# A retention block and a bilinear FFN in one kernel: the first regular group's queries and keys transposed by DMA instead of on TensorE, with the loads around it reordered

## The chip, the cores and the metric

The kernel runs on one core of a Trainium2 chip. The metric is the device time of one execution in microseconds (us). Before the change it is 326.99 us, the median of three runs (326.97 to 328.62).

## The reference

Inputs are q, k and v of shape [8, 8, 576, 64] (batch, heads, sequence, head dimension) and three FFN weights. The retention part computes scores, multiplies them with a causal decay, and applies them to v; there is no softmax. Its output, 4608 tokens of 512 channels, goes through a bilinear FFN.

```python
scores = scale * np.matmul(q, k.transpose(0, 1, 3, 2))
gamma = 1.0 - 2.0 ** (-5.0 - np.arange(H, dtype=np.float32))
Dmat = np.where(rel >= 0, gamma[:, None, None] ** rel[None, :, :], 0.0)
attn = np.matmul(scores * Dmat[None], v)          # [B, H, S, D]
x = attn.transpose(0, 2, 1, 3).reshape(B * S, H * D)
out = ((x @ w_a) * (x @ w_b)) @ w_out             # 512 -> 1536 -> 512
```

## The kernel before

**The FFN is the stream that everything else is woven into.** The 4608 tokens are worked off in blocks of 512, 256, 256 and then 512 tokens (line 111). For one block `ffn_block` runs, for each of 12 slices F of the hidden dimension, four matmuls into `pa` (L748) and four into `pb` (L763). ACT copies pa out of PSUM as `ha` (L756), and DVE multiplies ha with pb into `hT` (L768). Then, for each 128 tokens of the block (u = 0, 1, ...), twelve matmuls with `wo_sb` make `po` (L782), which ACT (L791) or DVE (L793) copies into an output buffer `osb`. There are four osb buffers. SP, the DMA queue of SyncE, stores them (L704, L706).

**Retention.** Tokens come in 18 groups of 256. Groups 0 to 2 are done in half-size steps at the start (STEPS, `transpose_step`, `score_step`, `output_step`); from group 3, the first regular one (FIRST = 3), each group passes these stages:

- `load_pair(n, which)` (L148): for q, k and v two DMAs of 256 KB each on SP's queue, into float32 stage tiles qf, kf, vf.
- `ahead(n)`: POOL casts q and k to bf16 `qkb` (L469, L473) and scales v into `vb` (L474).
- the transposition of qkb into `qkT`: by `turn(n)`, two transposing DMAs on SP's queue, one for q and one for k (L501); or, for group 3 alone, by `turned(3, part)`, four steps of four transposing matmuls on PE each (L492) into a PSUM tile of the FFN's own pool, and a copy to SBUF on ACT or DVE (L494).
- `stretch(into, outof)`: on PE, the states' part of the output of group `outof` (L627), the key-value sums of group `into` (`keyed`, L537, needs qkb and vb), its scores (`matched`, L599, needs qkT), and the keys' part of the output of `outof` (L640). DVE adds the sums (L562), masks the scores (L608) and scales the output into `xT` (L650), the FFN's input; ACT converts the states (L566, L569, L573). These are queued in `later` and emitted by `pop()` between FFN steps. `open_alone` and `close_outputs` do the two output parts without a new group.

**What sets the order.** The order is written by hand. `todo` is a list of (place, function, arguments); the place is counted in units of a 512-column matmul chain of PE from the FFN's start, so the first block takes 0 to 144, the second 144 to 216, the third 216 to 288, the fourth 288 to 432. At each edge of `ffn_block` all entries whose place has come are emitted, in the order of their places. Every engine, and SP's queue, works its instructions strictly in that order. So an entry that waits on SP also holds the loads and stores that stand behind it.

Two buffers matter for the change. The first block's four osb tiles are stored partly late: those of u = 0, 2 and 3 are put into `held` and stored by `store_held` entries, that of u = 1 is stored at once. The next block's osb tiles take the buffers that these stores free. And qkT has three buffers, as have qkb and vb.

Of the kernel before, what the change touches and what calls it, by code (L numbers as in the profile page):

```python
# [11 lines left out]
BF16 = mybir.dt.bfloat16  # L12
# [6 lines left out]
def kernel(  # L19
# [10 lines left out]
    nc = tc.nc  # L30

    B, H, S, D = q.shape
    DM = H * D
# [4 lines left out]
    HP = H // 2  # L38
# [8 lines left out]
    FIRST = 3  # L47
# [16 lines left out]
    def rows_of(n):  # L64

        if n not in LEFT:
            b, m = PAIRS[n]
            return [(kp, 0, 128, b, 256 * m + 128 * kp) for kp in (0, 1)]
        return [(i // 2, 64 * (i % 2), 64, 4 * LEFT[n] + i, S - 64)
                for i in range(4)]  # L70

    def pool(name, bufs, space=None):
        kw = {} if space is None else {"space": space}
        return ctx.enter_context(tc.tile_pool(name=name, bufs=bufs, **kw))
# [6 lines left out]
    qkt_pool = pool("qkt", 3)  # L81
# [7 lines left out]
    ps_ffn = pool("ps_ffn", 4, PS)  # L89
# [50 lines left out]
    def load_pair(n, which=(0, 1, 2)):  # L140
        if n >= NP:
            return
        paired.setdefault(n, {})
        for i in which:
            name, src = (("qf", q), ("kf", k), ("vf", v))[i]
            t = stage.tile([128, 2 * DM], FP32, tag=name, name=name + "2")
            for kp, r0, m, b, s0 in rows_of(n):
                nc.sync.dma_start(  # L148
                    t[r0:r0 + m, kp * DM:(kp + 1) * DM]
                    .rearrange("p (h d) -> p h d", h=H),  # L150
                    src[b, :, s0:s0 + m, :].rearrange("h s d -> s h d"))
            paired[n][i] = t

    def load_step(n, hh, which, on=nc.sync):

        if n not in paired:
            paired[n] = [stage.tile([128, 2 * DM], FP32, tag=name, name=name)
                         for name in ("qf", "kf", "vf")]
        on.dma_start(  # L159
            paired[n][which][:, hh * DM:(hh + 1) * DM]  # L160
            .rearrange("p (h e) -> p h e", h=4),
            (q, k, v)[which][n, 4 * hh:4 * hh + 4, 0:256, :]
            .rearrange("h (p two) d -> p h (two d)", two=2))

    STEPS = [(0, 0), (1, 0), (0, 1), (1, 1), (2, 0), (2, 1)]
    Q, K, V = 0, 1, 2
# [12 lines left out]
    identity = const.tile([128, 128], BF16)  # L179
# [49 lines left out]
    def pair_tables(step):  # L229
# [17 lines left out]
        else:  # L247
# [6 lines left out]
                for n in range(FIRST)]  # L254
    second = sum_pool.tile([128, FIRST, HP, 64], FP32, tag="sums",
                           name="second")
# [16 lines left out]
    natural, transposed, scored = {}, {}, {}  # L273
# [205 lines left out]
            op=ALU.mult)  # L479
        natural[FIRST + n, "pair"] = (qkb, vb)  # L480

    def turned(n, part):

        qkb = of(natural, n)[0]
        if part == 0:
            transposed[FIRST + n, "pair"] = qkt_pool.tile(
                [128, 2, 2, HP, 128], BF16, tag="qkT", name="qkT2")
        w, kp = part // 2, part % 2
        tp = ps_ffn.tile([128, HP, 128], BF16, tag="ab", name="tp2")
        for c in range(HP):  # L490
            e0 = kp * DM + c * 128
            nc.tensor.transpose(tp[:, c, :], qkb[:, w, e0:e0 + 128], identity)  # L492
        copy = (nc.scalar.copy, nc.vector.tensor_copy)[kp]
        copy(of(transposed, n)[:, w, kp], tp)  # L494

    def turn(n):
        qkb = of(natural, n)[0]
        qkT = qkt_pool.tile([128, 2, 2, HP, 128], BF16, tag="qkT",
                            name="qkT2")
        for w in (0, 1):  # L500
            nc.sync.dma_start_transpose(  # L501
                qkT[:, w].rearrange("p k c s -> p (k c) s"), qkb[:, w])
        transposed[FIRST + n, "pair"] = qkT
        if n == 9:
            load_pair(n + 1, (K, V))
        if n >= 9:
            load_pair(n + 2)

    def of(store, n):
        return store[FIRST + n, "pair"]  # L510
# [373 lines left out]
    nc.sync.dma_start(gate, wo_sb[0:1, 3, 0:64])  # L884
    for i, which in ((4, Q), (4, K), (4, V), (5, Q), (5, K), (5, V)):
        load_step(*STEPS[i], which)
    for n in (FIRST, FIRST + 1):
        load_pair(n)
    load_pair(FIRST + 2, (Q,))

# [20 lines left out]
    def turn_step(i):  # L913
# [3 lines left out]
    todo = [(100, early_casts, ()), (112, turn_step, (4,)),  # L917
            (112.1, cast_step, (5, Q, "act")), (116, score_step, (4,)), (116, state_step, (4,)),
            (124, turn_step, (5,)), (128, output_step, (4,)),
            (128, score_step, (5,)), (128, state_step, (5,)),  # L920
            (140, output_step, (5,))]
# [1 line left out]
    todo += [(136, total_of, (2,))]  # L923
    todo += [(28 + 6 * step, pair_tables, (step,)) for step in range(13)]
    todo += [(170, stretch, (3, None)), (197, stretch, (4, 3)),
             (240, stretch, (5, 4)), (272, open_alone, (5,)),
             (276, close_outputs, (5,)), (336, stretch, (6, None)),
             (372, stretch, (7, 6)), (408, stretch, (8, 7))]
    for n in range(8, NP, 2):
        todo += [(starts[n] - 116, stretch, (n + 1, n)),  # L930
# [2 lines left out]
                 (starts[n] - 44, open_alone, (n + 1,))]  # L933
    todo += [(starts[NP - 2] - 40, close_outputs, (NP - 1,))]
    placed = {args[0]: at for at, fn, args in todo if fn is stretch}
    casts = {3: 116, 4: 116, 5: 141, 6: 200, 7: 250, 8: 330}
    turns = {4: 116, 5: 145, 6: 240, 7: 338, 8: 345}
    loads = {7: 212, 8: 271, 9: 345.1}
    todo += [(345.2, load_pair, (10, (Q,))),
             (145.1, load_pair, (6, (K,))),  # L940
             (145.2, load_pair, (6, (Q,))), (145.3, load_pair, (6, (V,)))]
    for n in range(9, NP):
        casts[n], turns[n] = placed[n] - 70, placed[n] - 38
    todo += [(156 + 3 * part, turned, (3, part)) for part in range(4)]
    for fn, places in ((ahead, casts), (turn, turns), (load_pair, loads)):
        todo += [(at, fn, (n,)) for n, at in places.items()]
    todo += [(116, load_pair, (5, (K,))), (116, store_held, ()),
             (116, load_pair, (5, (V,))), (145, store_held, ())]
    todo.sort(key=lambda e: e[0])

    at = 0.0
# [40 lines left out]
```

## Time and profile before

| What | Value |
|---|---|
| Median of three runs | 326.99 us (326.97 to 328.62) |
| The profiled execution's own time | 327.43 us |
| Span of its instructions | 325.7 us |
| PE busy (matmul) | 319.4 us, 98% |
| DVE / ACT / POOL busy | 161.8 / 129.4 / 116.8 us |
| Granted TensorE clock | 1.0 in every stage |
| DMA, mean over the span | 155 GB/s; 66.7% of 16 engines in the main queue |
| SP's waits for stores of osb (L706 on ACT's copies) | 91.5 us in 13 waits |

All durations below are of the profiled execution. Times on the axis are counted from the start of its span. A matmul's busy time overlaps that of the next, so PE's timeline shows a group of four 256-column matmuls as 0.60 us although the next group starts 0.44 us later; the chain of waits shows the 0.44. A releaser (what an instruction waited for) is inferred from the last semaphore event; where the named one had long been done, it was another, often a DMA. For a DMA the profile tells when SP issued it, how long the issue held SP, and how long after the issue's start it landed.

### The profile page before, as it was taken

What the parts mean: (1) busy time and instruction counts of PE and PEld (TensorE: products, weight loads), DVE (VectorE), ACT (ScalarE), POOL (GpSimd) and SP (SyncE); (2) the same over time, 40 slices, a digit from 0 to 9 for tenths busy, and PEclk for the clock granted to TensorE, in tenths of its full rate; (3) what the DMA queues carried; (4) which work ended last, traced back from release to release, by engine and by line L of the source; (5) the groups of instructions that cost most, each with busy time, mean ns of one, the idle gap of its engine ahead of it and who ended that gap; (6) DMA issues with size and microseconds to landing.
All of it is one profiled execution on the core that took longest, in us unless ns stands there. A gap on an engine that the chain in (4) does not pass through costs nothing.

```text
span 325.7 us, 8666 instructions
## 1 busy us (share of the span) xinstructions
PE 319.4 (98%) x3615; PEld 165.1 (51%) x3615; DVE 161.8 (50%) x289; ACT 129.4 (40%) x286; POOL 116.8 (36%) x150
## 2 busy tenths in 40 slices
PE   7899999999999999999999999999999999999996
PEld 3564458768544554544454545454445444444443
DVE  5734455666446663845374626561556245314421
ACT  6845753563435523533253324442333233213321
POOL 4990078550876182757075205440520000000000
PEclk9999999999999999999999999999999999999999
DMA  8999999999999999996999169926840500031013
GB/s 216 254 197 207 262 225 223 191 176 202 221 220 221 215 231 198 209 210 152 194 199 189 51 159 200 217 62 149 206 67 31 140 28 0 2 97 32 3 29 100
DMA packets 143175, 50.37 MB, mean 155 GB/s; under 512 B 124576, under 2 KB 138656, under 8 KB 143136
## 3 DMA queue, kind: packets, MB, share of 16 engines
q1 hardware_dynamic: 137856, 44.84, 66.7%
q0 software_dynamic: 4752, 4.72, 8.8%
q8 instruction: 28, 0.46, 0.6%
q10 hardware_dynamic: 528, 0.26, 0.3%
q14 instruction: 11, 0.09, 0.1%
HBM read 37.75 MB, written 9.44 MB: 145 GB/s over the span
## 4 chain that ended last, share of the span: by engine, by line
PE 94%; DMA 2%; SPq 2%; ACT 1%; DVE 0%; issue 0%; DVEq 0%; ACTq 0%
PE po L782 29%; PE pb L763 29%; PE pa L748 28%; DMA qf<-in_q_dram 2%; SPq L159 2%; PE o L627 2%; PE o L640 2%; PE sc L599 1%; PE kv L537 1%; PE pa L725 1%; PE o L427 0%; PE kv L368 0%; PE sc L343 0%; PE tp L492 0%; PE tp L328 0%
## 5 line engine op out<-in xcount | busy, mean ns | idle before, releaser
L768 DVE TENSOR_TENSOR hT<-ha,pb 128x512 bf16<-128x512 bf16 (+1 forms) x120 | 75.9, 634 | 98.1 <-PE pb L763 90.9
L756 ACT CAST ha<-pa 128x512 bf16<-128x512 f32 (+1 forms) x120 | 64.8, 543 | 119.6 <-PE pa L748 116.4
L763 PE MATMUL pb<-xT,wb_sb 128*128 128x512 bf16 (+1 forms) x480 | 111.5, 358 | 0.3 <-ACT osb L791 0.3
L748 PE MATMUL pa<-xT,wa_sb 128*128 128x512 bf16 (+1 forms) x468 | 108.8, 357 | 0.0
L782 PE MATMUL po<-wo_sb,hT 128*128 128x512 bf16 (+2 forms) x444 | 97.5, 374 | 0.0
L763 PEld LDWEIGHTS <-wb_sb 128*128 128x128 bf16 x480 | 46.9, 98 | 47.0 <-issue 0.7
L748 PEld LDWEIGHTS <-wa_sb 128*128 128x128 bf16 x468 | 44.9, 98 | 44.3 <-issue 0.2
L782 PEld LDWEIGHTS <-hT 128*128 128x128 bf16 x444 | 41.9, 98 | 47.2
L469 POOL CAST qkb<-qf 64x1024 bf16<-64x1024 f32 x15 | 15.5, 1031 | 75.3 <-DMA qf<-in_q_dram 74.3
L474 POOL TENSOR_TENSOR vb<-vf,vs 128x1024 bf16<-128x1024 f32 x15 | 28.5, 1902 | 11.5 <-DMA vf<-in_v_dram 5.2
L793 DVE COPY osb<-po 128x512 f32<-128x512 f32 (+1 forms) x16 | 10.9, 683 | 39.7 <-PE po L782 39.7
L791 ACT COPY osb<-po 128x512 f32<-128x512 f32 (+1 forms) x21 | 12.0, 571 | 45.2 <-PE po L782 44.7
L650 DVE TENSOR_TENSOR xT<-o,qs 128x512 bf16<-128x512 f32 x30 | 19.5, 683 | 5.2 <-PE o L640 5.2
L562 DVE TENSOR_TENSOR sums<-kv,sums 128x256 f32<-128x256 f32 x44 | 18.6, 424 | 2.8 <-PE kv L537 0.8
L469 POOL CAST qkb<-kf 64x1024 bf16<-64x1024 f32 x15 | 15.8, 1052 | 11.4 <-DMA kf<-in_k_dram 10.8
L608 DVE TENSOR_TENSOR sT<-sc,mask 128x512 bf16<-128x512 f32 x30 | 19.5, 682 | 0.0
L473 POOL CAST qkb<-kf 64x512 bf16<-64x512 f32 x30 | 17.7, 616 | 0.8
L473 POOL CAST qkb<-qf 64x512 bf16<-64x512 f32 x30 | 17.6, 616 | 0.6
L566 ACT CAST states<-sums 64x512 bf16<-64x512 f32 x26 | 16.0, 617 | 0.3
L311 POOL CAST qkb<-kf 128x512 bf16<-128x512 f32 x5 | 3.1, 617 | 16.6 <-DMA kf<-in_k_dram 16.6
L667 ACT COPY fence<-o 128x2 f32<-128x2 f32 x15 | 2.4, 160 | 16.4 <-PE o L627 16.4
L809 PE MATMUL w<-ones 128*128 128x512 bf16 x19 | 7.0, 486 | 1.5 <-DVE idxp_f L204 1.5
(87 smaller groups left out, 163.1 us busy)
## 6 DMA issues: line engine op xcount, KB each, us to landing
qf<-in_q_dram SPq DMA_DIRECT2D x32, 256.0 KB, 5.2
vf<-in_v_dram SPq DMA_DIRECT2D x32, 256.0 KB, 5.1
kf<-in_k_dram SPq DMA_DIRECT2D x31, 256.0 KB, 4.9
out_dram<-osb SPq DMA_DIRECT2D x25, 256.0 KB, 2.9
out_dram<-osb SPq DMA_DIRECT2D x20, 128.0 KB, 2.4
wo_sb<-in_moe_w_out_dram POOLq DMA_DIRECT2D x3, 512.0 KB, 16.3
qf<-in_q_dram SPq DMA_DIRECT2D x8, 128.0 KB, 3.2
kf<-in_k_dram SPq DMA_DIRECT2D x8, 128.0 KB, 3.6
```

The source lines that it names most:

```text
L469: nc.gpsimd.tensor_copy(qkb[0:64, w], t[0:64])
L473: nc.gpsimd.tensor_copy(to[:, :, 1 - r], fro[:, :, r])
L474: nc.gpsimd.tensor_tensor(vb.rearrange("p (k h d) -> p k h d", k=2, h=H), vf.rearrange("p (k h d) -> p k h d", k=2, h=H), vs2[:, 2 if n in ...
L562: nc.vector.tensor_tensor(sums[:, i], own, prev, op=ALU.add)
L566: nc.scalar.copy(to(half(1 - r)), fro(half(r)))
L608: nc.vector.tensor_tensor(sT[:, on].rearrange("p c k s -> p (c k) s"), sc[:, on].rearrange("p c k s -> p (c k) s"), mask3.unsqueeze(1).to_ ...
L650: nc.vector.tensor_tensor(x_of(t0, 128).rearrange("p c (a s) -> p c a s", a=2), o[:, :, :, kp].rearrange("p a c s -> p c a s"), qs[:, :, s ...
L748: nc.tensor.matmul(pa[:, 0:n], wa_sb[:, c, fs], xT[:, c], start=(c == 0), stop=(c == NC - 1))
L756: nc.scalar.copy(ha[:, 0:n], pa[:, 0:n])
L763: nc.tensor.matmul(pb[:, 0:n], wb_sb[:, c, fs], xT[:, c], start=(c == 0), stop=(c == NC - 1))
L768: nc.vector.tensor_tensor(hT[:, F, 0:n], has[F][:, 0:n], pb[:, 0:n], op=ALU.mult)
L782: nc.tensor.matmul(po[:, 0:width], hT[:, F, u * 128:(u + 1) * 128], wo_sb[:, F, cols], start=(F == 0), stop=(F == NF - 1))
```

## The change

Group 3 is no longer transposed on PE: `turned` is deleted, and `turn(3)` puts two transposing DMAs on SP's queue at place 116. Because SP works in order, the loads around it are placed anew:

- Before the FFN's first block only group 3 and group 4's q are loaded ahead. Group 4's k and v come after `turn(3)`, then `turn(4)`, then group 5's q and k, the first `store_held`, and group 5's v.
- SP's order from group 3's loads on was: q3 k3 v3, q4 k4 v4, q5, turn 4, k5, store of u = 0, v5, store of u = 1, turn 5. It becomes: q3 k3 v3, q4, turn 3, store of u = 1, k4 v4, turn 4, q5 k5, store of u = 0, v5, turn 5.
- The stretch of groups 5 and 4 moves from place 240 to 248, two FFN slices later. `open_alone(5)` and `close_outputs(5)` move from 272 and 276 to 274 and 278; since the next edges are 276 and 280, each comes four po matmuls later.
- `turn(7)` moves from 338 to 272. On SP it then stands right after group 8's q, and group 8's k and v come after it, with one output store between.

```diff
-    def turned(n, part):
...
-        tp = ps_ffn.tile([128, HP, 128], BF16, tag="ab", name="tp2")
-        for c in range(HP):
-            e0 = kp * DM + c * 128
-            nc.tensor.transpose(tp[:, c, :], qkb[:, w, e0:e0 + 128], identity)
-        copy = (nc.scalar.copy, nc.vector.tensor_copy)[kp]
-        copy(of(transposed, n)[:, w, kp], tp)
...
-    for n in (FIRST, FIRST + 1):
-        load_pair(n)
-    load_pair(FIRST + 2, (Q,))
+    load_pair(FIRST)
+    load_pair(FIRST + 1, (Q,))
...
-             (240, stretch, (5, 4)), (272, open_alone, (5,)),
-             (276, close_outputs, (5,)), (336, stretch, (6, None)),
+             (248, stretch, (5, 4)), (274, open_alone, (5,)),
+             (278, close_outputs, (5,)), (336, stretch, (6, None)),
...
-    casts = {3: 116, 4: 116, 5: 141, 6: 200, 7: 250, 8: 330}
-    turns = {4: 116, 5: 145, 6: 240, 7: 338, 8: 345}
-    loads = {7: 212, 8: 271, 9: 345.1}
-    todo += [(345.2, load_pair, (10, (Q,))),
+    casts = {3: 116, 4: 116.15, 5: 141, 6: 200, 7: 250, 8: 330}
+    turns = {3: 116, 4: 116.2, 5: 145, 6: 240, 7: 272, 8: 345}
+    loads = {7: 212, 9: 345.1}
+    todo += [(345.2, load_pair, (10, (Q,))), (271, load_pair, (8, (Q,))),
+             (272.1, load_pair, (8, (K, V))),
...
-    todo += [(156 + 3 * part, turned, (3, part)) for part in range(4)]
...
-    todo += [(116, load_pair, (5, (K,))), (116, store_held, ()),
-             (116, load_pair, (5, (V,))), (145, store_held, ())]
+    todo += [(116.1, load_pair, (4, (K, V))), (116.3, load_pair, (5, (Q, K))),
+             (116.4, store_held, ()), (116.5, load_pair, (5, (V,))),
+             (145, store_held, ())]
```

More of the change, by code (lines that the diff above doesn't have):

```diff
@@ L480, in ahead @@
         natural[FIRST + n, "pair"] = (qkb, vb)
-    def turned(n, part):
[L484 to L488, printed above, removed]
-        tp = ps_ffn.tile([128, HP, 128], BF16, tag="ab", name="tp2")
-        for c in range(HP):
-            e0 = kp * DM + c * 128
-            nc.tensor.transpose(tp[:, c, :], qkb[:, w, e0:e0 + 128], identity)
-        copy = (nc.scalar.copy, nc.vector.tensor_copy)[kp]
-        copy(of(transposed, n)[:, w, kp], tp)
     def turn(n):
```

## The prediction

> **What bounds the kernel now.** I read part 1 of the page first: PE is busy almost all the span.
>
> ```profile
> PE 319.4 (98%) x3615; PEld 165.1 (51%) x3615; DVE 161.8 (50%) x289; ACT 129.4 (40%) x286; POOL 116.8 (36%) x150
> PE 94%; DMA 2%; SPq 2%; ACT 1%; DVE 0%; issue 0%; DVEq 0%; ACTq 0%
> ```
>
> The second line, the chain that ended last, says the same: 94% of it is matmuls. So an edit is worth what it takes from, or puts into, PE's stream. I then asked for the chain between 50 and 80 us, where the diff acts (start, duration, what):
>
> ```profile
> 53.31 0.22 PE tp L492 x4
> ...
> 65.18 0.32 PE sc L599 x32
> ...
> 69.78 0.45 PE pb L763 x4
> 70.23 0.04 issue
> 70.27 0.59 ACT osb L791
> 70.87 0.04 issue
> 70.91 0.60 PE pb L763 x4
> ```
>
> Here are one of the four transposing steps of group 3, and one of the few places where PE waits: a pb matmul is held by ACT's copy of an output block (osb). The copy begins only at 70.27. ACT's timeline says why:
>
> ```profile
> 69.08 0.82 ACT L566 CAST left_states<-sums 64x256 bf16<-64x256 f32 x2
> 70.27 0.59 ACT L791 COPY osb<-po 128x512 f32<-128x512 f32 x1 [0.38 <-PE pb L763]
> ```
>
> ACT is free at 69.90 and idles 0.37 us, although its po matmuls ended at 69.35. What it wants is an osb buffer: there are four, the first four belong to the 512 tokens before, and SP stores those late. SP's timeline (one queue, strictly in order):
>
> ```profile
> 46.41 2.74 SPq L148 DMA_DIRECT2D qf<-in_q_dram  x2
> 49.26 2.19 SPq L148 DMA_DIRECT2D kf<-in_k_dram  x2
> 51.63 1.82 SPq L148 DMA_DIRECT2D vf<-in_v_dram  x2
> 53.55 2.19 SPq L148 DMA_DIRECT2D qf<-in_q_dram  x2
> 55.85 4.73 SPq L501 DMA_TRANSPOSE qkT<-qkb  x2
> 60.63 1.26 SPq L148 DMA_DIRECT2D kf<-in_k_dram  x2
> 61.99 2.13 SPq L704 DMA_DIRECT2D out_dram<-osb  x2
> 64.16 1.31 SPq L148 DMA_DIRECT2D vf<-in_v_dram  x2
> 65.57 2.39 SPq L704 DMA_DIRECT2D out_dram<-osb  x2
> 68.07 2.85 SPq L501 DMA_TRANSPOSE qkT<-qkb  x2
> ```
>
> The stores issued at 65.57 and 66.40 take 4.3 and 3.8 us to land (tile osb in that window), so the last lands at 70.2: just before the copy starts. SP is never idle here, and the page's slices show 190 to 225 GB/s throughout. SP and the transfers behind it are a second bound, hidden under PE by a small margin. The change takes work from the first and puts it on the second.
>
> **Removed from PE.** Four steps of four transposes, 0.22 us each on the chain: **-0.88 us**. The four copies at L494 (0.59 on ACT, 0.42 on DVE) go too; beside them PE waited for nothing, so they are worth 0. From here PE would meet the scores of group 4 (65.18 before) at 64.30.
>
> **Added to SP.** Nothing changes until group 4's q is issued (ends 49.15). Then come T3 (two transposing DMAs), the second output block's two stores, k4 and v4, T4, q5 and k5, the first block's two stores, v5, T5.
> - T3. Group 3's k is cast by 50.55 (POOL: 49.37 + 1.18), so SP waits at most about 1 us, inside the issue time. Pairs of transposes took 2.72 (at 91.42) to 4.73 us of SP's time; the row at 55.85 also stands in a full queue. I take 3.5: SP is free at 52.75. Its second half is issued near 51.1 and lands 4.2 us later (as the half issued at 58.39 did), at 55.3; its scores come at 58.07 - 0.88 = 57.19, so 1.9 us cover it. If that cover is gone, PE waits one for one.
> - Two stores: rows of 2.13 and 2.39, and 1.40 at 81.31. I take 1.9: 54.65.
> - k4. From the issue at 60.63 to POOL's cast at 65.55 the same pair took 4.92; so POOL casts k4 from 59.6, not 55.39.
> - Cast: 65.55 to 67.82, 2.27 us: 61.9. The second transpose of T4 waits for it, and everything on SP behind: it is issued at about 62.0. vb (1.90) is ready at 63.8; PE wants it at 64.03.
> - It lands 3.5 us later (median of the 28; they go from 3.2 to 5.4): 65.5. PE wanted it at 64.30: **+1.2 us** of waiting before the scores, where before it had landed by 62.6 (58.39 + 4.2), 2.6 us early.
>
> Both ends of this chain: with the shortest rows T4's second half is issued at 60.7 and lands at 63.9, no wait; with the longest, 63.6 and 69.0, a wait of 4.7.
>
> [...] The rows: a pair of transposes of 8 tiles each has landed 6.7 us after its first issue (55.85 to 62.6), and costs SP 3.5 against 1.26 for two loads (60.63). [...]
>
> **The store that frees the buffer.** In the new order the second block is stored before the first, near 53 instead of 65.6. osb buffers come free in the order of the stores, so the first copy of the next 256 tokens (66.79) now meets landed stores, and the second one (70.27) takes the buffer of the first block, whose stores stand behind T4, q5 and k5. T4 is issued by 63.3 (62.0 + 1.3). Four loads follow, at 256 KB and some 215 GB/s 1.2 us apart (an estimate from the slices), the first 3.6 us after its issue: the fourth lands at 70.6. The two stores land behind, 0.35 us apart as at 69.9 and 70.2: 71.3. The copy runs 71.4 to 72.0, and pb, at 70.91 before, starts at 72.05. In PE's timeline the pa before it starts at 70.06 and a pb follows 0.44 later, so free of the buffer pb would have been at 70.50, and now at 70.50 - 0.88 + 1.2 = 70.82. So this wait is 1.23 instead of 0.41: **+0.82**. The bounds move with T4's second issue: one us later there is one us here.
>
> **Moved edits costed at 0.** The stretch of groups 5 and 4 goes behind two more pairs of ffn steps (2 x 0.87). T5's second half: stores and v5 end at 70.8, k5's cast at 73.0, so it lands near 76.6; PE now needs it at 75.64 + 1.14 + 1.75 = 78.5. At the old place it would have been 76.8, hardly covered. The bubble after that stretch (77.24 to 78.99 on the chain, some 0.6 us lost, hT and sums on DVE) is in both; bounds -0.6 to +0.6. open_outputs(5) and close_outputs(5) move behind four more po matmuls each: after L640 DVE needs 1.29 for two scalings (85.78) plus 0.2 of starts, while eight po matmuls cover 1.73; at worst +0.3. SP ends T5 some 3.5 us later than 70.9; T6, landed by 96.1 (92.85 + 3.3), comes to 99.6, and its scores, 99.08 before, are due at 100.2: covered by 0.6, at worst +1.5. Group 7's T goes ahead of k8 and v8: its matmuls at 108.71 were covered by only about 0.4 (103.97 + 4.3), and are now covered by several us. Behind it, SP waits for output copies before 121 anyway and takes up the delay.
>
> **Sum.** -0.88 + 1.2 + 0.82 = **+1.14 us**. The profiled execution took 327.43 (span 325.7 and 1.73 around it), so it would be 328.57. That execution lies 0.44 above the median of 326.99; against the median I predict **328.1**. One half per cent, 1.63 us, is about what a measurement of this kernel can tell from no change.
>
> **Rivals.**
> - *Slower by over 0.5%.* The same late store with a longer queue: each us by which T4's second transpose is issued after 62.0 is a us at the pb matmul. From 62.5 on the loss is above 1.63. For it: pairs of transposes of 4.7 us, stores of 2.39 and a landing of 5.4 are all in the trace, and any wait at T6 adds to it. With issue at 63.5: 1.14 + 1.5 = +2.6, 329.6. Against it: it needs rows from the long half twice. Chance 0.37.
> - *The transposes' time stays saved.* SP has room: T3 costs 2.7, stores 1.4, T4's second issue is at 60.7, its landing meets PE, and stores are not held by the loads ahead. Then -0.88 and the 0.41 go: 325.7; with the stores in line still -0.1. Only with the DVE bubble gone too (-0.6) is it faster by over 0.5%. Against it: SP and the transfers show no idle time from 33 us on. Chance 0.13, 0.06 of it past 0.5%.
> - *The new transposes come too late themselves* (the change doesn't take group 3 off PE's path): T3 landing after 57.2 puts a wait where the transposes were. 1.9 us speak against it; it would also push T4, so it is counted in the first rival.
>
> **How the numbers follow.** The forecast case (+0.1 to +1.6, 327.1 to 328.6) has 0.50, the first rival 0.37, the second 0.13. Faster 0.06, within 0.5% 0.50 + 0.07 = 0.57, slower 0.37. The range leaves out about 1 in 10 on each side: from 326.5 (half of the saving kept) to 330.1 (+3.1: T4's second issue near 64).
>
> **What would show it.** L492 gone from the chain; SP at T3 from about 49 to 53; POOL's k4 cast near 59.6 instead of 55.4; PE waiting about 1 us in front of sc L599 near 65 with a DMA as releaser; ACT's second osb copy near 71.4, still held by a store; no wait at the scores of groups 5, 6 and 7. I am wrong if the copy at L791 starts as soon as its po is done, or if T4's second half lands before 64.3: then the change gains. I am also wrong if a stretch further on (group 5 or 6) shows the new wait.

## The result, and the profile after

The changed kernel takes 328.34 us (median of 22 runs, 327.90 to 330.86) against 327.34 us for the kernel before beside it (22 runs, 326.96 to 328.62). The ratio is 1.0033, 95% interval 1.0023 to 1.0043: one microsecond slower, which lies within the half per cent. The forecast was 328.1. The profiled execution of the kernel after took 327.9 us (span 326.2); it is the shortest of its 22 runs, so its trace may show the loss at its mildest.

All line numbers behind L481 are 14 lower than before, because `turned` is gone: osb copies are L777, pa L734, pb L749, the transposing DMAs L487, kv L523, the scores L585.

The page of the kernel after, parts 1 and 4 and one group of part 5 (busy time and mean ns of one; then the idle time just before, and what ended most of it), and below it the same group on the page of the kernel before:

```profile
PE 318.7 (98%) x3599; PEld 164.4 (50%) x3599; DVE 161.9 (50%) x287; ACT 128.4 (39%) x284; POOL 116.3 (36%) x150
PE 91%; DMA 3%; ACT 2%; SPq 1%; DVE 1%; POOL 1%; issue 1%; ACTq 0%; DVEq 0%; POOLq 0%
L749 PE MATMUL pb<-xT,wb_sb 128*128 128x512 bf16 (+1 forms) x480 | 111.5, 358 | 1.4 <-ACT osb L777 1.3
```

```profile
L763 PE MATMUL pb<-xT,wb_sb 128*128 128x512 bf16 (+1 forms) x480 | 111.5, 358 | 0.3 <-ACT osb L791 0.3
```

PE has sixteen instructions fewer (3599, not 3615), the transposes. Yet PE's share of the chain that ended last fell from 94% to 91%: the shares of DMA, ACT and DVE have grown, and POOL has entered it. The third line says where the largest piece is: pb matmuls waited 1.3 us for ACT's copies of osb, and 0.3 us before.

The chain of the kernel after around that place (start, duration, what):

```profile
56.57 5.74 DMA vf<-in_v_dram
...
62.47 1.91 POOL vb L474
64.38 0.04 issue
64.42 0.45 PE kv L523 x32
...
66.45 0.60 ACT osb L777
67.05 1.09 SPq L690
68.14 0.04 issue
68.18 2.70 DMA out_dram<-osb
...
70.98 0.59 ACT osb L777
71.58 0.04 issue
71.62 0.60 PE pb L749 x4
```

Before the change this stretch was matmuls up to 70.27. Now it goes from the load of group 4's v over POOL to the key-value products, and then over SP's queue and a store to the osb copy at 70.98. (The osb copy at 66.45 stands in this chain only as an inferred releaser: the store carries the FFN's first output block, u = 0, which ACT had copied by 40.87; it stood on SP behind other DMAs.) ACT's timeline of the kernel after confirms the second part: ACT was free at 69.55 and idle for 1.43 us, until a store had landed.

```profile
68.73 0.82 ACT L552 CAST left_states<-sums 64x256 bf16<-64x256 f32 x2
70.98 0.59 ACT L777 COPY osb<-po 128x512 f32<-128x512 f32 x1 [1.43 <-DMA out_dram<-osb]
```

SP's timeline of the kernel after (start, time that the issues held SP) shows the store's place:

```profile
48.86 4.01 SPq L487 DMA_TRANSPOSE qkT<-qkb  x2
52.97 1.18 SPq L690 DMA_DIRECT2D out_dram<-osb  x2
54.20 1.32 SPq L148 DMA_DIRECT2D kf<-in_k_dram  x2
55.56 1.91 SPq L148 DMA_DIRECT2D vf<-in_v_dram  x2
57.64 4.99 SPq L487 DMA_TRANSPOSE qkT<-qkb  x2
62.67 1.25 SPq L148 DMA_DIRECT2D qf<-in_q_dram  x2
63.97 1.97 SPq L148 DMA_DIRECT2D kf<-in_k_dram  x2
66.03 2.74 SPq L690 DMA_DIRECT2D out_dram<-osb  x2
```

The new pair of transposes is the line at 48.86. The two stores of the first output block (u = 0; below, "the first block's stores"), the last line, are issued at 66.03 and 68.18, behind the second pair of transposes and four loads.

**Where the time went, by the profiles.** The pa before the late pb starts at 69.72 on PE's timeline, and a pb follows 0.44 later: it was due at 70.16 and came at 71.62, so 1.46 us late instead of 0.41. At group 4's key-value products PE lost 0.28 us more (on PE's timeline, from the second block's first po to its sixteenth, with group 4's stretch between, it took 4.87 instead of 4.59 us). With the transposes gone: -0.88 + 1.05 + 0.28 = +0.45. On the clock of the profiles, from the first pa of the FFN's second block to that of its fifth (PE's timeline) it is 72.29 us before (50.53 to 122.82) and 72.62 after (50.80 to 123.42): +0.33. I call these 72.3 us the touched stretch. From there to the last block both take the same 168.40.

### The profile page after: what moved, and what is told of

It is laid out like the page before. It is cut to its first block, busy times and chain, and to the rows that moved or that the text cites. A ratio compares the mean times of both kernels' runs of the same rounds, so it can differ in the third digit from the quotient of the medians.

```text
span 326.2 us, 8627 instructions
## 1 busy us (share of the span) xinstructions
PE 318.7 (98%) x3599; PEld 164.4 (50%) x3599; DVE 161.9 (50%) x287; ACT 128.4 (39%) x284; POOL 116.3 (36%) x150
## 4 chain that ended last, share of the span: by engine, by line
PE 91%; DMA 3%; ACT 2%; SPq 1%; DVE 1%; POOL 1%; issue 1%; ACTq 0%; DVEq 0%; POOLq 0%
PE po L768 28%; PE pb L749 27%; PE pa L734 26%; DMA vf<-in_v_dram 2%; PE o L613 2%; PE o L626 2%; PE w L795 1%; PE sc L585 1%; PE kv L523 1%; PE tp L328 1%; DMA out_dram<-osb 1%; PE pa L711 1%; SPq L148 1%; SPq L690 1%; POOL vb L474 1%; PE o L427 1%
## 5 line engine op out<-in xcount | busy, mean ns | idle before, releaser
L749 PE MATMUL pb<-xT,wb_sb 128*128 128x512 bf16 (+1 forms) x480 | 111.5, 358 | 1.4 <-ACT osb L777 1.3
L734 PE MATMUL pa<-xT,wa_sb 128*128 128x512 bf16 (+1 forms) x468 | 108.8, 357 | 0.0
L749 PEld LDWEIGHTS <-wb_sb 128*128 128x128 bf16 x480 | 46.9, 98 | 48.0 <-issue 1.7
L734 PEld LDWEIGHTS <-wa_sb 128*128 128x128 bf16 x468 | 45.0, 98 | 44.4 <-issue 0.2
L777 ACT COPY osb<-po 128x512 f32<-128x512 f32 (+1 forms) x21 | 12.0, 571 | 47.2 <-PE po L768 45.8
```

The source lines that it names most:

```text
L734: nc.tensor.matmul(pa[:, 0:n], wa_sb[:, c, fs], xT[:, c], start=(c == 0), stop=(c == NC - 1))
L749: nc.tensor.matmul(pb[:, 0:n], wb_sb[:, c, fs], xT[:, c], start=(c == 0), stop=(c == NC - 1))
```

## The experiments

Each line of the table is a kernel of this section; the ratio is to the kernel before, measured beside it (its medians there: 327.34 to 327.62 us), and need not be the quotient of two medians. "Stretch" is the touched stretch in the one profiled execution.

| Kernel | Median us | Ratio (95%) | Stretch us |
|---|---|---|---|
| before | 327.34 | | 72.29 |
| after | 328.34 | 1.0033 (1.0023 to 1.0043) | 72.62 |
| e1_store_behind_t4 | 328.33 | 1.0034 (1.0021 to 1.0047) | 73.46 |
| e2_store_behind_v5 | 333.18 | 1.0173 (1.0151 to 1.0194) | 77.29 |
| e3_pe_transposes_new_order | 327.25 | 0.9998 (0.9990 to 1.0007) | 72.06 |
| e4_later_places_alone | 327.40 | 1.0002 (0.9993 to 1.0011) | 71.91 |
| e5_earlier_places | 328.51 | 1.0031 (1.0019 to 1.0043) | 73.72 |
| e6_before_store_first | 327.14 | 0.9976 (0.9952 to 1.0001) | 71.95 |
| e7_loads_k4v4_first | 327.50 | 1.0001 (0.9987 to 1.0015) | 72.96 |
| e8_stores_by_act | 338.36 | 1.0344 (1.0322 to 1.0366) | |
| e9_before_stores_by_act | 342.79 | 1.0466 (1.0451 to 1.0482) | |
| f1_waits_cleared | 327.61 | 0.9994 (0.9975 to 1.0013) | 71.41 |
| f2_same_with_pe_transposes | 327.60 | 1.0001 (0.9988 to 1.0014) | 72.10 |
| f3_transposes_before_store | 327.55 | 0.9997 (0.9985 to 1.0010) | 71.53 |

**e1_store_behind_t4: the late store earlier.**

```diff
-             (116.4, store_held, ()), (116.5, load_pair, (5, (V,))),
+             (116.25, store_held, ()), (116.5, load_pair, (5, (V,))),
```

> The changed kernel with the first block's two stores put right behind group 4's transposing DMAs, ahead of group 5's q and k; nothing else. Late-store theory: the stores land near 66.5 instead of 70.9, ACT's second osb copy starts when ACT is free (69.6), the pb matmul that was held (71.62) starts near 70.2, about 1.4 us are won: ratio to before 0.9985 to 0.9995 instead of 1.0033. Rival (group 4's k, v and transposes come too late): unchanged, 1.003. Rival (30 transposing DMAs instead of 28 slow every transfer a little): unchanged, 1.003.

The time is that of the kernel after. The wait itself did go: in ACT's timeline the copy starts as soon as ACT is free, with no idle time shown.

```profile
69.23 0.57 ACT L777 COPY osb<-po 128x512 f32<-128x512 f32 x1
```

But PE's timeline of the same kernel has three waits that the kernel after did not show (the bracket is the idle time, and what ended it):

```profile
64.51 0.45 PE L585 MATMUL sc<-qkT 64*64 64x64 bf16 x32 [0.16 <-DMA qkT<-qkb]
...
77.03 0.45 PE L523 MATMUL kv<-vb,qkb 64*64 64x64 bf16 x32 [0.89 <-POOL vb L474]
...
99.93 0.45 PE L585 MATMUL sc<-qkT 64*64 64x64 bf16 x32 [0.60 <-DMA qkT<-qkb]
```

The first is group 4's scores, which wait for T4: the wait that the prediction forecast, much smaller. The second is group 5's values, whose load now stands behind the stores; the third is group 6's transposes. So the late store is a wait that can be taken away by itself, and not the reason for the loss as a whole.

**e2_store_behind_v5: the same store later.**

```diff
-             (116.4, store_held, ()), (116.5, load_pair, (5, (V,))),
+             (116.6, store_held, ()), (116.5, load_pair, (5, (V,))),
```

> The changed kernel with the first block's two stores put behind group 5's v, two loads later than now. Late-store theory: two loads of 1.2 us go ahead of the stores, so the copy and the pb matmul come 2 to 2.5 us later, one for one: ratio 1.0095 to 1.011. Rival (group 4's data late): the stores don't matter, 1.003. Rival (transfers slower in general): the same number of bytes, 1.003.

Direction right, size too small. PE's timeline:

```profile
75.34 1.01 PE L749 MATMUL pb<-xT,wb_sb 128*128 128x256 bf16 x4 [3.95 <-ACT osb L777]
76.15 1.06 PE L734 MATMUL pa<-xT,wa_sb 128*128 128x256 bf16 x4
77.00 1.06 PE L749 MATMUL pb<-xT,wb_sb 128*128 128x256 bf16 x4
```

The store is on the path: moving it behind one load of two DMAs adds 2.65 us of waiting at pb (3.95 instead of 1.30). More came on top: the groups behind the wait follow each other in 0.85 us instead of 0.44. The windows of this kernel give the reason (the window and its length, the busy time of PE, PEld, DVE, ACT and POOL, then the granted clock, DMA's share and GB/s):

```profile
71.30:75.30 4.00, 0.10 (x1) 0.00 (x0) 0.00 (x0) 0.59 (x2) 3.80 (x6) 0.93 0.93 208
75.30:78.60 3.30, 3.25 (x18) 2.41 (x18) 1.27 (x3) 0.92 (x3) 1.38 (x1) 0.57 0.77 165
```

PE does next to nothing for 4 us, and then its granted clock is 0.57 for 3.3 us, which costs about 1.3 us (three groups at 0.4 more each, and part of a fourth).

**e3_pe_transposes_new_order: the new order without the new transposes.** The kernel after, with `turned` on PE again and no transposing DMAs for group 3:

```diff
-    turns = {3: 116, 4: 116.2, 5: 145, 6: 240, 7: 272, 8: 345}
+    turns = {4: 116.2, 5: 145, 6: 240, 7: 272, 8: 345}
+    todo += [(156 + 3 * part, turned, (3, part)) for part in range(4)]
```

> The changed kernel with group 3 transposed on TensorE again, so SP's new order without the two added transposing DMAs. Late-store theory, with the two DMAs as what makes the store late: SP is 4 us earlier from 49 us on, the stores land near 67, no wait for the buffer, none for vb of group 4, and the 0.88 us of PE are back: 0.4 us better than before, ratio 0.9985 to 0.9995. Rival (the new order alone is to blame): the waits stay and 0.88 comes on top, 1.005 to 1.006.

0.9998, against 1.0033 with the DMAs. In its profile PE's timeline names no wait from 50 to 125 us, and the osb copy starts as soon as ACT is free:

```profile
69.98 0.57 ACT L791 COPY osb<-po 128x512 f32<-128x512 f32 x1
```

So the loss comes from the two transposing DMAs in the new order, not from the new order by itself. Whether it is their issuing on SP or their transfers that makes the rest late, this kernel doesn't tell. The small gain that I expected, 0.41 us from the osb wait of before, is hardly there (0.02%); e6 comes back to it.

**e4_later_places_alone and e5_earlier_places: the retimed entries.** e4 is the kernel before with only the later places; e5 is the kernel after with only these undone.

```diff
-             (240, stretch, (5, 4)), (272, open_alone, (5,)),
-             (276, close_outputs, (5,)), (336, stretch, (6, None)),
+             (248, stretch, (5, 4)), (274, open_alone, (5,)),
+             (278, close_outputs, (5,)), (336, stretch, (6, None)),
```

(e4 also has `turn(7)` at 272 and group 8's load split, as in the change.)

> The kernel before with only the parts that the prediction costed at nothing: the stretch of groups 5 and 4 two slices later, open and close of group 5 later, group 7's transposes and group 8's loads as in the change. My theory: 0, ratio 0.999 to 1.001, no new wait at the scores of groups 5, 6, 7. Rival (these places carry part of the loss, by the scalings of group 5 coming late for the next block): plus 0.3 to 0.5 us, 1.001 to 1.0015.

> The kernel after with one edit undone: group 5's stretch at 240 and its open and close at 272 and 276 again, as in the kernel before (248, 274 and 278 in the kernel after). Our theory: the queue of SP is late by the two transposing DMAs of group 3, so group 5's transposes land at about 76.5 and its values are ready at about 75.5 in the profile of after; eight steps earlier the scores are due at about 76.3 and the key-value products at about 76.0, so a wait of 0.1 to 0.3 us comes in and the ratio to the kernel before is 1.0035 to 1.0045. Rival: the retiming itself is what costs the time (through the DVE bubble or the outputs of group 5), and without it the ratio falls back to 1.000 to 1.002.

e4 is at 1.0002, e5 at 1.0031 and so not told apart from the kernel after (1.0033). So what was costed at nothing is nothing that these intervals can tell; e5 lies below the range of its theory and above that of its rival. In e5's profile the cover is in fact gone, as the prediction said it would be ("hardly covered"): its scores of group 5 wait 0.56 us for their transposes at 76.94, which the kernel after does not show; within the intervals that does not move the time.

**e8_stores_by_act and e9_before_stores_by_act: the stores off SP's queue.** In the kernels after and before:

```diff
-                    nc.sync.dma_start(rows[par::2], osb[half(par), cols])
+                    on = nc.scalar if n == 0 else nc.sync
+                    on.dma_start(rows[par::2], osb[half(par), cols])
```

> The kernel after with the stores of block 0's tokens issued by ACT's queue instead of SP's; no byte more or less is moved. Theory that SP's issuing is the limit: four stores leave SP's queue (about 1.2 us for the first pair and 2.7 us for the second), group 4's loads and transposes come some 1 us sooner, the waits for osb (1.46) and for the values of group 4 (0.30) go, and the saving of 0.88 shows: about 326.6, ratio 0.997 to 0.9985. Rival, the transfers themselves (bytes in flight) are the limit, whichever queue issues them: ratio 1.002 to 1.0035. Second rival: the issuing on ACT, about 2 us ahead of its copies for TensorE, holds TensorE up there, and the ratio is above 1.003.

> The kernel before with the same edit: block 0's stores issued by ACT's queue. Theory that SP's issuing is the limit: its wait of 0.41 us for osb goes, ratio 0.9985 to 0.9995, and the transposing DMAs are then worth the rest of their 0.88 us between this kernel and the kernel after with the same edit (0.001 to 0.002 apart). Rival, transfers are the limit: ratio 0.9995 to 1.0005.

The second rival came true, far beyond its size. ACT's timeline of e8, then PE's, then DVE's, and last the chain of waits that led there:

```profile
50.38 6.69 ACTq L691 DMA_DIRECT2D out_dram<-osb  x4
57.11 0.59 ACT L330 COPY qkT<-tp 128x512 bf16<-128x512 bf16 x1 [12.18 <-DMA out_dram<-osb]
```

```profile
57.75 0.64 PE L343 MATMUL sc<-qkT 64*64 64x128 bf16 x16 [10.27 <-ACT qkT L330]
```

```profile
44.95 0.68 DVE L780 COPY osb<-po 128x512 f32<-128x512 f32 x1
```

```profile
50.23 6.34 DMA qkT<-qkb
56.58 0.02 issue
56.60 0.47 ACTq L691
57.07 0.04 issue
57.11 0.59 ACT qkT L330
```

ACT worked in order too: a copy that PE needed stood behind the four stores (ACT was idle for 12.18 us before it, 15.74 in e9), and PE was idle for 10.27 us. The stores did not wait for what they store. ACT had written the one output block by 41.86 and DVE the other by 45.63. By the chain above the last of the four issues began at 56.60, just after a transposing DMA of SP's queue had landed (56.58), and held ACT for 0.47 of the 6.69 us. In e9's chain ACT's queue is released at 55.86, just after a v load of SP's queue has landed (55.84). Why an issue by ACT waits for a DMA of SP's queue, the trace does not show. These two kernels tell what it costs to put an issue that waits in front of work; they say nothing on whether SP's issuing or the transfers themselves are the limit. That stays open.

**e7_loads_k4v4_first: both late transfers earlier.** e1 with group 4's k and v earlier as well:

```diff
-    todo += [(116.1, load_pair, (4, (K, V))), (116.3, load_pair, (5, (Q, K))),
-             (116.4, store_held, ()), (116.5, load_pair, (5, (V,))),
+    todo += [(116, load_pair, (4, (K, V))), (116.3, load_pair, (5, (Q, K))),
+             (116.25, store_held, ()), (116.5, load_pair, (5, (V,))),
```

> The kernel after with only the order of SP's queue changed: k and v of group 4 at the head of the step (116), and the stores of the first block ahead of group 5's q and k (116.25). Theory of the queue as a whole: SP has no slack from 48 to 100 us, so no order wins; what the first block's stores gain, group 5's and 6's transposes lose, and the ratio stays at 1.002 to 1.0035. Rival, one late store: with the store early and the values of group 4 early, the two waits of the kernel after (1.46 and 0.30 us) are both gone and the ratio is 0.9975 to 0.999.

1.0001, between the two theories. Order alone wins back the microsecond that the change lost, so my theory that no order can win fell. But it doesn't go below the kernel before either. PE's timeline shows what is late next, group 5's values and group 6's transposes:

```profile
77.04 0.45 PE L523 MATMUL kv<-vb,qkb 64*64 64x64 bf16 x32 [1.19 <-POOL vb L474]
...
99.52 0.45 PE L585 MATMUL sc<-qkT 64*64 64x64 bf16 x32 [0.28 <-DMA qkT<-qkb]
```

**f1_waits_cleared, f2_same_with_pe_transposes, f3_transposes_before_store: those waits covered too.** f1 is e7 with group 5's stretch one slice later and group 6's transposes ahead of group 7's v. f2 is f1 with group 3 on PE. f3 is f1 with group 6's transposes between group 7's load and the next stores. f1 against e7, then f3 against f1:

```diff
-             (248, stretch, (5, 4)), (274, open_alone, (5,)),
+             (252, stretch, (5, 4)), (278, open_alone, (5,)),
...
-    turns = {3: 116, 4: 116.2, 5: 145, 6: 240, 7: 272, 8: 345}
-    loads = {7: 212, 9: 345.1}
+    turns = {3: 116, 4: 116.2, 5: 145, 6: 212.1, 7: 272, 8: 345}
+    loads = {9: 345.1}
+             (212, load_pair, (7, (Q, K))), (212.2, load_pair, (7, (V,))),
```

```diff
-    turns = {3: 116, 4: 116.2, 5: 145, 6: 212.1, 7: 272, 8: 345}
-    loads = {9: 345.1}
-             (212, load_pair, (7, (Q, K))), (212.2, load_pair, (7, (V,))),
+    turns = {3: 116, 4: 116.2, 5: 145, 6: 212, 7: 272, 8: 345}
+    loads = {7: 211.9, 9: 345.1}
```

> The kernel of the last call with group 4's k and v and the first block's stores early (1.0001), and two edits more: group 5's stretch at 252 and its open at 278, so that its key-value products meet values that are ready (they waited 1.19 us there), and group 6's transposing DMAs ahead of the load of group 7's v (its scores waited 0.28 us). No instruction is added. Theory of places, each wait of the changed kernel is one late transfer that another order covers: both waits go, the saving of 0.88 us on TensorE shows, ratio 0.9960 to 0.9980. Rival, SP's queue as a whole has no room for the two transposing DMAs: the lateness turns up at another product or store, ratio 0.9990 to 1.0010.

> The kernel f1_waits_cleared with group 3's transposes on TensorE again (places 156 to 165, sixteen products, as in the kernel before) and without its two transposing DMAs. If the saving of 0.88 us is real once the waits are covered, this one is 0.6 to 1.0 us above f1_waits_cleared, ratio 0.9990 to 1.0005. Rival, the DMAs cost as much as they save wherever they stand: no more than 0.3 us above f1_waits_cleared, or below it.

> The kernel f1_waits_cleared with group 7's load whole again and group 6's transposing DMAs behind it, ahead of the stores that follow (f1_waits_cleared had them ahead of group 7's v, and its profile then showed 0.57 us of wait at group 8's scores and 0.33 us at group 5's outputs). Theory of places: the 0.57 us goes, the 0.33 us stays, so 0.88 - 0.33 = 0.55 us under the kernel before, ratio 0.9975 to 0.9990. Rival, the lateness of SP's queue is a spread from run to run that no single profile shows: some other product or store waits in other runs, ratio 0.9990 to 1.0010.

The two waits that f1 was to cover are gone, and its touched stretch is 71.41 us, 0.88 under before. That this equals the saving on PE is chance, since the osb wait of before (0.41) is gone too and a new wait of 0.33 has come. f2, which has the transposes on PE and the same new wait, takes 72.10, that is 0.69 more. f1 then loses 0.57 us further on, at group 9's scores (f3's expectation calls them group 8's). Their transposes landed at 130.11, no later than in e7 (130.74), but PE came for them at 129.58, where in e7 it came at 131.00. So the lateness turned up elsewhere, as f1's rival said; PE's timeline of f1:

```profile
130.15 0.45 PE L585 MATMUL sc<-qkT 64*64 64x64 bf16 x32 [0.57 <-DMA qkT<-qkb]
```

f3's PE timeline doesn't name that wait; the only one between 60 and 132 us is this, which f1 has as well.

```profile
86.27 0.45 PE L626 MATMUL o<-sT,vb 64*64 64x64 bf16 x32 [0.33 <-ACT fence L653]
```

That f3's order covers group 9 is not shown by it: the transposes landed at 130.29, later than in f1, and the scores came at 130.55 because PE was late from the start. f3's profiled execution reached the second block only at 51.50 (50.53 before), and those 0.97 us are there already at the FFN's first matmul (17.44 against 16.46), in code that these kernels share.

The times don't follow the touched stretch: f1, f2 and f3 are at 0.9994, 1.0001 and 0.9997, where the rivals had them, and f2's median is that of f1. A late start can hide f3's gain of 0.76 in one run, but hardly in a median of twelve. The runs of f1 and f3 spread over 2.5 and 1.9 us. That fits waits which one execution shows and another not.

The profiles do show such waits where the order is the same. The kernel after, e1, e2 and e5 have one order on SP up to group 4's transposes; in their profiled executions group 4's stretch cost 0.28, 0.48, 0.95 and 0.73 us more than before (from the second block's first po to its sixteenth, 4.59 us before). And before and e4 have one order up to the osb copy at 70 us, where only before waits. That this is what holds the medians of f1 and f3 up is argued, since no trace of their longer runs was taken. Whether the 0.88 us can be had stays open: f1's interval is 0.38% wide, more than the 0.27% that is looked for, and f3's ends at 0.9985, so f3's gain is at most some 0.5 us.

**e6_before_store_first: the wait that stood in the kernel before.** The kernel before, with v of group 5 behind the stores of u = 0 and of u = 1:

```diff
-              (116, load_pair, (5, (V,))), (145, store_held, ())]
+              (120.5, load_pair, (5, (V,))), (145, store_held, ())]
```

> The kernel before with one place changed: v of group 5 at 116 instead of 120.5, so behind the first block's stores of step 116 and no longer between group 4's transposes and the second pair of stores. Our sum took the 0.41 us that ACT's second copy into osb waits in the profile of before as a fixed part of its time: then the ratio is 0.9985 to 0.9995. Rival: that wait stands in some executions only, being as long as the transfers happen to run late, and the ratio is 0.9995 to 1.0005.

(The expectation has the two places the wrong way round: 116 is that of the kernel before, and 120.5 is e6's, which puts the load behind the stores of both.)

0.9976, with an interval from 0.9952 to 1.0001 that reaches no change. Its median lies 0.48 us under that of the kernel before beside it (by the two medians 0.9985; three of the 29 runs of before took 329.89 us or more), and its eleven runs spread over only 0.53 us (326.93 to 327.46). Its profile has no wait at that copy. That speaks for the fixed part. e4's profile speaks for the rival: it has the old order of the stores and no wait at that copy. Of all kernels of the table it has the shortest median, and it keeps the transposes on TensorE; that it beats the kernel before is not shown.

## Why the prediction was right, and where it was not

- **-0.88 on PE: right.** L492 is gone, and the second block's twelve slices are shorter by the four steps (11.44 instead of 12.34 us from the first block's last po to the second block's first).
- **T3 itself in time: right.** SP is at the new transposes from 48.86 to 52.87 (forecast 49 to 52.75; 4.01 instead of 3.5 us). Group 3's scores do not wait. The rival of T3 coming too late is refuted: the last of the sixteen tiles landed at 54.84, 5.98 us after the first issue. From issue to landing the transposing DMAs of the kernel after are not slower than its loads: the median is 3.8 us for the 30 transposing DMAs and 4.9 to 5.1 us for the loads of 256 KB. SP's time is another matter: 4.01 us for this pair, against 1.32 for the two loads at 54.20.
- **The two added DMAs cost more than the 0.88 that they save: right**, shown by e3. That their place in SP's order decides how much is shown by e7, which keeps them and is level with before. That SP's issuing is the limit, and not the transfers behind it, is not shown.
- **The store of the first output block: right in place, mechanism and nearly in size.** Forecast: landed 71.3, copy 71.4, a wait of 1.23. Measured: landed 70.88, copy 70.98, a wait of 1.46. The term is +1.05 instead of +0.82. (The prediction's 190 to 225 GB/s between 50 and 80 us are 176 to 223 in the page's slices of before, with 176 from 65.1 to 73.3 us.)
- **"+1.2 us of waiting before the scores": mis-sized, and it is another wait.** T4's second half was issued at 61.40 and landed at 64.52 (forecast 62.0 and 65.5), just before the scores at 64.68. POOL's cast of k began at 59.10, not 59.6:

```profile
59.10 1.03 POOL L469 CAST qkb<-kf 64x1024 bf16<-64x1024 f32 x1 [4.22 <-DMA kf<-in_k_dram]
60.20 1.17 POOL L473 CAST qkb<-kf 64x512 bf16<-64x512 f32 x2
62.47 1.90 POOL L474 TENSOR_TENSOR vb<-vf,vs 128x1024 bf16<-128x1024 f32 x1 [1.10 <-DMA vf<-in_v_dram]
```

  POOL then idled 1.10 us for v, which landed at 62.31, so vb was ready at 64.38 and not at the forecast's 63.8. The key-value products, one step ahead of the scores, lost 0.28. I had followed k and not v, which stands two issues behind it on the queue. Without that wait the scores would have come at about 64.40, just before T4; in e1 and e2, with the same order up to there, they do wait for it, 0.16 and 0.18 us.
- **Moved edits at 0: right as far as the times can tell** (e4 and e5). That group 5 would be "hardly covered" at the old place was right too: 0.56 us late in e5's profile.
- **The sum.** +1.14 forecast; +0.45 from the waits of the profiled execution, +1.00 between the medians. That 328.1 lies so close to 328.34 is in part luck: in the profile group 4 cost 0.9 less than forecast and the osb copy 0.2 more. This profile is of the shortest run, and in e1, e2 and e5 group 4 cost 0.48 to 0.95, which would bring the sum to +0.65 to +1.12; but no trace of a longer run of the kernel after shows where the rest of its median comes from.
- **"One us later there is one us here": too mild.** e2's wait of 3.95 us cost some 1.3 us more than itself, while the granted clock was at 0.57.
- **What the prediction did not see:** that the late store was only the first of several late transfers. It had T6 covered by 0.6 us and did not price group 5's values by themselves. With the store out of the way (e1), waits of 0.16, 0.89 and 0.60 us stand at groups 4, 5 and 6, nearly as much as the 1.46 and 0.28 of the kernel after.

## What to carry to other kernels

Work taken off the busiest engine can be worth nothing if it goes onto an in-order queue that has no slack (here 0.88 us off PE, and the kernel 1.00 us slower): price it by what stands behind it on that queue, each store and load with the time at which its reader needs it, and not only by the first one that is late. Taking one such wait away can move it to the next late transfer, as e1 did (0.16, 0.89 and 0.60 us at groups 4, 5 and 6), so follow the queue on until one is covered. And where runs of a kernel spread by more than the gain that is looked for, one profile can be its best case: here it was the shortest of 22.

## What the runs showed that was not expected

- After a gap of 3.95 us in PE's work its granted clock was 0.57 for 3.3 us in e2, with groups of four matmuls 0.85 us apart instead of 0.44, about 1.3 us lost on top. After the gap of 1.30 us of the kernel after (PE's timeline; the 1.46 are against the time that was due) the clock stayed at 1.00 (its windows from 69.70 to 75.00). After the 10.27 us gap in e8 it was 0.50 from 58 to 62 us, 0.82 up to 65.5 and 1.00 from there. Where between 1.30 and 3.95 us the change comes, these three gaps do not tell.
- Four stores of 128 KB kept ACT from its work for 12.18 us in e8, although their data were there by 45.63: the last was issued at 56.60, just after a transposing DMA of SP's queue had landed (56.58). In the kernel after, the same four took 1.18 and 2.74 us of SP's time.
